# A second tile for the transposed probabilities, three copies with a second engine to run on, and a new order for the first 800 tasks

## The chip, the cores and the metric

The kernel runs on one core of a Trainium2 chip. The metric is the device time of that core in microseconds: 615.44 us, the median of three runs before the change (614.84 to 616.58).

## The reference, cut to what matters

Block attention with a local window and block summaries, followed by a two-layer feed-forward net with softplus. `q`, `k`, `v` are 4 x 8 x 768 x 64 in fp32.

```python
k_sum = k.reshape(B, H, nb, 32, D).max(axis=3)      # 24 block summaries of the keys
v_sum = v.reshape(B, H, nb, 32, D).mean(axis=3)
scores_l = where(|i - j| < 16, scale * q @ k.T, -1e9)
scores_s = scale * q @ k_sum.T + log(32)
a = softmax(concat[scores_l, scores_s])
x = (a @ concat[v, v_sum]).transpose(...).reshape(3072, 512)
h = x @ w_in                                        # 512 x 2048
out = softplus(h) @ w_out                           # 2048 x 512
```

## The kernel before, in words

The 3072 tokens are twelve chunks of 256, taken in six groups x of two chunks. All matrix products of the net run as three products of rounded fp32 halves (a high part and a low part of each operand), so every weight and every x is split once into "high" and "low". The 2048 hidden features f are 16 tiles of 128. The first pass takes tiles 0 to 7 for groups 0 to 4, the last group takes all 16, then tiles 8 to 15 follow for groups 4 to 0.

The kernel body does not run its work directly. It adds 2052 numbered tasks to a list; each task has an engine, a function that emits its instructions and the tiles that it reads and writes. `SEQUENCE` is a string written out by hand with all task numbers, and `Order.issue` emits the tasks in that order. Each engine then runs its own tasks in exactly this order, and waits where a tile is not ready or not yet free. A letter behind a number picks another way for the task: "a" is the first entry of its list `ways`, "b" the second. The SP queue issues all DMAs, also in this order.

An attention unit is two head pairs of one chunk. The first group has four, called U1 to U4 here in the order of their numbers: U1 is tasks 59 to 72, U2 73 to 86, U3 97 to 110, U4 111 to 124. Each runs these tasks, given with U1's numbers: scores (59, PE, line 650), mask with the row's maximum (60, DVE, L663), exp with the row's sum (61, ACT, L671), inverse of the sum (62, DVE, L678 and L679), normalise (63, on POOL or DVE at L684, or on ACT at L687), two transposes on PE (64 and 66, L704), two copies of the transposed probabilities into the tile `pT` (65 and 67, L708), values (68, PE, L749), and for each head pair the high part of x (69 and 71, L777) and its low part (70 and 72, L781). All units share one `pT`. The units of later groups (U5 is tasks 298 to 315, U6 323 to 340) go another way from the normalised probabilities to `pT`: a block transpose on DVE into the tile `tb` (303 in U5, L717), a DMA out to memory (304) and four DMAs back into `pT` (305 to 308).

Beside this the weights are prepared in place, tile by tile: load, magnitude (L951 on DVE, L954 on ACT), clamp, shift, sign (L958 to L966, DVE), tail (L972 on ACT, L975 on DVE), add_tail (L980, POOL), high (L984) and low (L991). Tasks 132 to 167 are the four 512-column pieces of weight pair 0 (w_in from 132 and 150, w_out from 141 and 159, nine tasks each); 168 to 186 are pair 1, 187 to 205 pair 2 and 206 to 224 pair 3, each a w_in and a w_out piece of 1024 columns. Task 50 is the mean of the values' blocks (L441).

The first products of the net are tasks 225 and 226 (the two halves of hidden tile f0, L1077), 234 and 235 (f1), 241, 242, 248 and 249 (f2 and f3); 227, 228 and 229 are the softplus of f0 (rounded, exact and the rest, L1227, L1231, L1235), and 230 to 233 its four projections into the output tiles (L1242). 27 tasks (3 to 29, `warm`, L1316) multiply the identity by itself, two matmul records each; nothing reads their result.

The lines that the change touches:

```python
pT = buffer([P, NG * NU * P], F32, "pT", bufs=1)
order.add(ACT, act(NU * P, True), transposed, [pt], [(pT, g)])
order.add(ACT, act(CH, True), high, [xo], [(*key, 0, i)])
order.add(ACT, act(DM, True), mean, [total], [kept])
```

Of the kernel before, what the change touches and what calls it, by code (L numbers as in the profile page):

```python
# [10 lines left out]
F32 = mybir.dt.float32  # L11
# [3 lines left out]
AF = mybir.ActivationFunctionType  # L15
# [135 lines left out]
94 316 100 189 25 148a 190 26 151a 152 27 114 90 101b 155 149 153 92 95 191 68 71 69 154 78 91 96 299 80 156 79 81 177  # L151
82 300 178 157a 72 323 127 358 129 158 70 115a 160 102 341 104 83 345 128 85 161 103 86 162 301 84 105 192 28 29 106
164 107 109 302a 163 116 118 225 117 165 119 108 183 303 304 324 120 193 166 234 343 123 121 325 206 349 122 347 124
110 226 235 167a 342 292 353 346 179 180 475 326 476a 365 227 228 181 236 229 327b 237 230 344a 231 182 351 241 242
194 297 293 296 305 238 184 350 211 248 328 243 249 348a 244 185 232 294 250 186 233 251 239 366 352 308 329 307 306
367 295 240 245 383 196 252 246 197 354 130 195 207a 247 368 309 330 317 208 369b 479a 209 390 210 331 333 332 255 256
370 310 474 314 355 212 391 198a 320 322 262 392 213a 199 253 318 321 319 202a 200 371 214 215 393 263 482 254 201 257
216 258 264 259 203 265 334 394b 501b 266 269 359 360 356a 372 375 373 270 335 502b 505 357 204a 276 395 205a 500 363
217a 277 483 361 374 362 364 260 218 396 219 221 271 220 261 272 278 273 508 279 222 280 376 526 484 267 384 223a 397
400 399 224 268 398 387 312a 274 389 385 337 527b 313a 528b 485 388 339 486a 377 379 275 284 282 281 386 381 340a 648  # L160
487 382a 338a 488 509 283 510 652 126 401 315 533 380 536 402a 404a 406a 288 407 554 405 408 489 491 492 490 477 478
480 409 555b 410 556 649 511 417 512a 561a 411 285 286a 656 412 418 481 513 413 419 514 537 420 403 650 660 424 421
538 414 415 425 426 564 493 665 666b 427 667 651 289a 539 540a 541 416 515 503 504 517 422 516 506 428 423 518 494a
429 507 565 566 542 87 654 125 653 672 567 568a 430 431 432 433 519 543 529 434 657 435 675 520 524a 569 436 693 544
676 677 678 438 439 437 530 525 661 655 534 531 570 546 545 440 532 535 441 694 662 700a 442 445 446 496a 658 522 523
695 497a 443 447 448 449 679a 547 557 571 562 558 559 560 680 703 722 548 721 574 550 551a 704 573 563 572 723 659
663a 452 705 706 453 444 450 88 681 451 454 726a 707 457 455 456 729 747 748 752a 749b 575 576 578 498a 499a 459 708
552 580 553a 581 460 682 336 378 685 579a 582 461 462 463 495 583 730 458 584 585 287 465 290 668 670 466 464 311 683
664 467 468a 591 592 471a 897 469 731 586 669 587 709 674 684 598 732 733 755 577 593 588 734 840b 589 901 599 594 595
605 756 846 839 671 606 841b 600 601 607 602 849 472a 608 673 868a 895 609 686 590 596 735 869 710 757 758 612 613 696  # L170
699 898a 698 614 597 615 687 689 712 603 521 701 697 713 604 616 691a 711 702 899 714 867 896 903 715 619 759 620 724
760 850 610 851 736 725 739 737 611 900 852 874a 626 853 621 470 622 719 627 738 623 628 904 617 629 727 761 728 740
741 877 905 907 762 688 902 618 630 765 633 764 912 745 750 624 625 634 913b 753 751 631 763 754 632 854 717 906 766
878 914a 919 879 855 922 880 842 690 635 743a 856 940 908 636 848 473 881b 843 637 746 718a 720a 767a 771a 692 744
941b 857 847 845 769a 638 942a 772 859 770a 844 773 782 642a 774 858 775 882 776 923 883 783 784 947a 777 639 785 640
950 860 884 641 924 886 1035 786 645a 789 549 861a 870 887 646a 1034 643 873 1036 909 778 885 790 925 926a 779 875 876
871 927 951 796 780 952 791 1039a 953 797 792 781 862 742 793 910 787 954 798 799 863 872 788 794 928 888 800 1366 915
911 955 956 1042 889a 1043 1044 1045 1046 929 918 803 804 647 1047 810 811 805 812 921 931 916 1059b 813 806 1063a 865
920 932 1060 807 930 1058 795 801 802 808 644 917 1066 866 814 768 1067 893a 1083 933 943 957 934a 960 949 809 815 816
936 938a 1084a 946 1089a 864a 939 935 817 818 1068 948 1082 891a 892 819 820 944 824 825 821 958 959 822 826 945 1048  # L180
1069 961 827 962 1500 716 1092 1070a 1037 937 823 964a 1367 894a 966 828 1049 963 1052 829 1038 1041 1051 1071 833 967
965a 831 1109 968 832 969 970 1108 977 1040 971 890 836a 1115a 837 978 979 830 1050 980 1072 1093 1110 972 981 1118
1053 1094 834a 1061 973 1054 974 1095 1056 1057 1064 1062 1368a 1096 1055 1073 975 1065 1076 984 985 986 987 991 992
988 993 1097 1119 994 1075 838 976 998 999 1000 1501a 995 1074 1001 1002 1098 982 1077 1372 835 1369 1120 1121 1078
1080 1506 983 1085 1081 1099 1091 989 990 1079 1005 1006 1502 1100 1012 1007 1102 1376 1008 1122b 996 1086 1088 1087
1090 1009 997 1123 1013 1101 1103 1014 1124 1015 1106 1003 1111 1004 1113 1016 1112 1019 1373 1104 1125 1020 1379 1010
1021 1117 1128 1022 1023 1127 1107 1116 1114 1503 1011 1126 1017 1510 1105 1507a 1018 1025 1026 1129 1024 1130 1132
1131 1028 1031 1133 1134 1135 1143 1136 1144 1027 1137 1145 1138 1192 1029 1139 1150 1151 1146 1193a 1147 1157 1210
1152 1032 1158 1211 1140 1212 1141 1194 1228 1195 1196 1213 1159 1153 1142 1160 1154 1161 1215a 1148 1214 1233 1201
1164 1149 1171 1172 1165 1229 1206a 1377a 1216 1197 1155 1033 1156 1217 1162 1219 1247 1030 1202a 1230 1231 1203 1232  # L190
1220a 1204 1205 1207 1198 1166 1234 1167 1173 1199 1163 1237 1218 1168 1174 1200a 1175 1178 1179 1248a 1249 1235 1185
1180 1181 1224a 1250 1169 1238 1170 1186 1251 1285 1236 1266 1182 1243 1252 1239a 1240 1221 1176 1241 1208 1242 1187
1253 1188 1177 1189 1302 1267a 1268 1183 1303 1222 1309 1244 1269 1290a 1310 1184 1256 1304 1305 1223 1306 1190 1311
1191 1257 1254 1271 1275 1225 1312 1313 1316 1226 1378a 1317 1323 1209 1270 1245 1255 1272 1227 1318 1319 1324 1307
1262 1325 1308 1273 1246 1314 1315 1276 1320 1286 1287a 1326 1277a 1258a 1327 1274 1330 1288 1259 1260 1281 1331 1261
1332 1333 1334 1337 1278 1263 1321 1338 1279 1344 1339 1380a 1345 1340 1322 1280 1341 1289 1351 1381 1352 1294a 1346
1374 1264 1375 1347 1265 1382 1328 1329 1370 1348 1371 1335 1336 1385 1282 1283 1383 1353 1354 1355 1386 1387a 1508a
1291 1384 1342 1388 1391 1389a 1392 1390 1394 1393 1395 1396 1399 1397 1284 1343 1398 1295 1292 1400 1403 1404 1401
# [33 lines left out]
def kernel(  # L232
# [111 lines left out]
    class Sums:  # L344
# [69 lines left out]
        def declare_first_values(self):  # L414
# [1003 lines left out]
```

## Time and profile before

| what | value |
|---|---|
| median of three runs | 615.44 us |
| span of the profiled execution, first to last instruction | 612.5 us |
| median less that span | 2.9 us |
| PE busy | 601.8 us (98%) |
| DVE, ACT, POOL busy | 383.8, 342.6, 179.3 us |
| granted TensorE clock, mean | 1.000 |

The span is that of one profiled execution; no time of its own beyond the span is given for it, and 2.9 us lie between the span and the median of the timed runs. PE counts as busy while a matmul waits in its pipeline, so 98% is not 98% of its rate: how much work a stretch holds is read from the number of matmuls in it.

### The profile page before, as it was taken

The numbers are of one execution on the slowest core, as the hardware profiler recorded it, in microseconds if no ns is written. First come the engines' busy times: TensorE is split into PE (matmuls) and PEld (weight loads), VectorE is DVE, ScalarE is ACT, GpSimd is POOL, SyncE is SP. The second block draws the span as 40 slices with busy tenths as digits, with TensorE's granted clock in tenths as the row PEclk, the third lists the DMA queues.
The fourth block names the chain that finished last, engine by engine and source line by source line (L and its number), as shares of the span: only waits on it lengthen the run. The fifth ranks groups of instructions, "written<-read, shape, count | busy, mean of one in ns | idle before, by whom it ended". The sixth has DMA issues, their size and how long they took to land.

```text
span 612.5 us, 12196 instructions
## 1 busy us (share of the span) xinstructions
PE 601.8 (98%) x4557; PEld 505.8 (83%) x4557; DVE 383.8 (63%) x990; ACT 342.6 (56%) x847; POOL 179.3 (29%) x179
## 2 busy tenths in 40 slices
PE   8899999999999999999999999999999999999997
PEld 7577878888788788888888888899898989899996
DVE  4999988765566665442235689854765665554543
ACT  4999998876778656576265986432213222133211
POOL 4324242244115132210003553572411236012000
PEclk9999999999999999999999999999999999999999
DMA  8989868988768476655428510041060043030121
GB/s 293 314 274 289 249 229 251 290 244 281 250 208 268 158 214 221 222 195 192 135 74 272 205 70 1 1 155 52 1 225 16 1 130 112 34 104 1 47 92 68
DMA packets 69130, 98.62 MB, mean 161 GB/s; under 512 B 6000, under 2 KB 47824, under 8 KB 68304
## 3 DMA queue, kind: packets, MB, share of 16 engines
q1 hardware_dynamic: 69072, 97.85, 49.9%
q8 instruction: 36, 0.59, 0.4%
q14 instruction: 22, 0.18, 0.1%
HBM read 67.11 MB, written 28.31 MB: 156 GB/s over the span
## 4 chain that ended last, share of the span: by engine, by line
PE 77%; ACT 10%; DVE 7%; DMA 2%; issue 2%; POOL 1%; SPq 0%; DVEq 0%; ACTq 0%; POOLq 0%
PE po L1242 36%; PE ph L1077 16%; PE hx L1117 10%; PE hy L1117 7%; PE xo L749 3%; PE sc L650 3%; PE warm L1316 2%; DMA raw<-w_out_dram 2%; ACT sp L671 1%; ACT raw L972 1%; ACT L1227 1%; ACT t L954 1%; DVE sp L663 1%; ACT L954 1%; ACT ph L1231 1%
## 5 line engine op out<-in xcount | busy, mean ns | idle before, releaser
L1242 PE MATMUL po<-w,gh 128*128 128x512 f32 x766 | 203.0, 392 | 0.7 <-DVE w L991 0.5
L1242 PEld LDWEIGHTS po<-w,gh 128*128 128x128 f32 x766 | 140.8, 188 | 30.3 <-DVE w L991 1.0
L1077 PE MATMUL ph<-xw,w 128*128 128x512 f32 x672 | 161.7, 391 | 0.0
L1077 PEld LDWEIGHTS ph<-xw,w 128*128 128x128 f32 x672 | 125.2, 188 | 27.2 <-issue 0.5
L1242 PE MATMUL po<-w,gl 128*128 128x512 f32 x383 | 114.5, 392 | 0.5 <-DVE gl L1235 0.5
L1242 PEld LDWEIGHTS po<-w,gl 128*128 128x128 f32 x383 | 70.7, 188 | 15.4 <-DVE gl L1235 0.9
L671 ACT ACTIVATE sp<-sp,nm 128x120 f32<-128x120 f32 x192 | 73.1, 386 | 4.2 <-DVE nm L663 4.0
L980 POOL TENSOR_TENSOR t<-t,raw 128x1024 int32<-128x1024 int32 (+1 forms) x20 | 40.7, 2042 | 111.1 <-DVE t L966 85.9
L1227 ACT ACTIVATE gh<-hx 128x512 fp32r<-128x512 f32 x20 | 12.0, 600 | 107.6 <-DVE hx L1127 107.6
L1235 DVE TENSOR_TENSOR gl<-ph,gh 128x512 fp32r<-128x512 f32 x56 | 38.4, 689 | 50.4 <-ACT ph L1231 50.1
L1227 ACT ACTIVATE gh<-ph 128x512 fp32r<-128x512 f32 x56 | 33.4, 598 | 38.3 <-PE ph L1077 38.1
L821 POOL TENSOR_TENSOR x<-r,x 128x512 fp32r<-128x512 f32 x23 | 30.5, 1338 | 53.2 <-DVE x L814 43.5
L663 DVE CUSTOM_DVE_ANT_0 sp<-sc,added 128x120 f32<-128x120 f32 x192 | 40.8, 277 | 4.1 <-PE sc L650 3.1
L671 ACT ACTIVATION_READ_ACCUMULATOR sp<-sp,nm 128x1 f32 x192 | 36.7, 191 | 0.0
L1117 PE MATMUL hx<-x,w 128*128 128x256 f32 x240 | 35.7, 285 | 0.0
L1117 PE MATMUL hx<-x,sw 128*128 128x256 f32 x240 | 35.5, 284 | 0.0
L1117 PEld LDWEIGHTS hx<-x,w 128*128 128x128 f32 x240 | 32.9, 190 | 2.1
L1117 PE MATMUL hy<-x,sw 128*128 128x256 f32 x240 | 34.4, 284 | 0.0
L1227 ACT ACT_TABLE_LOAD x23 | 29.5, 1283 | 6.2 <-PE ph L1077 5.8
L1231 ACT ACTIVATE ph<-ph 128x512 f32<-128x512 f32 x56 | 33.0, 591 | 0.0
L1117 PEld LDWEIGHTS hx<-x,sw 128*128 128x128 f32 x240 | 32.0, 190 | 0.8
L1117 PEld LDWEIGHTS hy<-x,sw 128*128 128x128 f32 x240 | 31.2, 191 | 0.2
(120 smaller groups left out, 831.7 us busy)
## 6 DMA issues: line engine op xcount, KB each, us to landing
squares<-tb SPq DMA_DIRECT2D x20, 512.0 KB
pT<-squares SPq DMA_DIRECT2D x80, 128.0 KB
raw<-w_out_dram SPq DMA_DIRECT2D x16, 512.0 KB
kf<-kT_dram SPq DMA_DIRECT2D x16, 384.0 KB
raw<-w_in_dram SPq DMA_DIRECT2D x6, 1024.0 KB
q<-qT_dram SPq DMA_DIRECT2D x20, 256.0 KB
part<-ob SPq DMA_DIRECT2D x10, 512.0 KB
out_dram<-ob SPq DMA_DIRECT2D x10, 512.0 KB
```

What stands on the lines that cost most here:

```text
L650: nc.tensor.matmul(unit(g * NU + h * NPAIR + i)[r * QW:(r + 1) * QW, k0:k1], lhsT=q[rows, w * QW:(w + 1) * QW], rhs=k[rows], start=True, s ...
L663: nc.vector.tensor_tensor_reduce(out=sp()[:, n], in0=unit(n), in1=added()[:, kinds.index((lows[w], lows[w + 1]))], scale=-SCALE, scalar=FL ...
L671: nc.scalar.activation(sp()[:, n], sp()[:, n], AF.Exp, bias=nm()[:, n:n + 1], scale=-1.0, accum_out=ss()[:, n:n + 1],)
L749: nc.tensor.matmul(xo()[h * D:(h + 1) * D, g * CH + w * QW:g * CH + (w + 1) * QW], lhsT=v[:, h * D:(h + 1) * D], rhs=queries(g, w, h), sta ...
L821: engine.tensor_tensor(to(1), a(), to(0).bitcast(F32), op=ALU.subtract)
L980: nc.gpsimd.tensor_tensor(a, a, word(0, I32), op=ALU.add)
L1077: nc.tensor.matmul(ph(), lhsT=lhs(part, cc), rhs=xw[cc][0]()[:, xw[cc][1], a], start=cc == 0 and n == 0, stop=cc == NCC - 1 and n == 2,)
L1117: nc.tensor.matmul(to()[:, half], lhsT=lhs(wa, cc), rhs=of_x(xa)[:, cc * CH:(cc + 1) * CH], start=cc == 0 and m == 0, stop=cc == NG - 1 an ...
L1227: nc.scalar.activation(gh(), all_of(), AF.Softplus)
L1231: nc.scalar.activation(all_of(), all_of(), AF.Softplus)
L1235: nc.vector.tensor_sub(out=gl(), in0=all_of(), in1=gh().bitcast(F32))
L1242: nc.tensor.matmul((to or po[t])()[:, c0:c1], lhsT=a()[:, t * P:(t + 1) * P], rhs=w2()[:, part, i2 * DM + c0:i2 * DM + c1], start=(f == f0 ...
```

## The change

Four edits. The tile of the transposed probabilities takes the ring of `tb` for the second chunk of the first group (U2 and U4), and stays in the ring of `pT` for U1 and U3. The copies out of the transposes, the high part of x in the first group (and in the last, which runs through the same code) and the mean of the values may also run on DVE. The first 800 places of `SEQUENCE` hold the same 800 tasks in another order and partly with other letters; the 1252 places behind them are the same.

```diff
-        pT = buffer([P, NG * NU * P], F32, "pT", bufs=1)
+        pT = buffer([P, NG * NU * P], F32, "pT", "tb" if by_pe and i else "pT", 1)
...
-                def transposed(g=g, pt=pt):
-                    nc.scalar.copy(out=pT()[:KS, g * NU * P:(g + 1) * NU * P], in_=pt()[:KS])
-                order.add(ACT, act(NU * P, True), transposed, [pt], [(pT, g)])
+                def transposed(copy, g=g, pt=pt):
+                    copy(out=pT()[:KS, g * NU * P:(g + 1) * NU * P], in_=pt()[:KS])
+                order.add(ACT, act(NU * P, True), lambda f=transposed: f(nc.scalar.copy), [pt], [(pT, g)], ways=[Way(DVE, dve(NU * P), lambda f=transposed: f(nc.vector.tensor_copy))])
...
-            order.add(ACT, act(CH, True), high, [xo], [(*key, 0, i)])
+            order.add(ACT, act(CH, True), lambda f=high: f(nc.scalar.copy), [xo], [(*key, 0, i)], ways=[Way(DVE, dve(CH), lambda f=high: f(nc.vector.tensor_copy))])
...
-            order.add(ACT, act(DM, True), mean, [total], [kept])
+            def mean_by_vector(): nc.vector.tensor_scalar_mul(kept()[KW:KS], total()[KW:KS], 1.0 / BLOCK)
+            order.add(ACT, act(DM, True), mean, [total], [kept], ways=[Way(DVE, dve(DM), mean_by_vector)])
```

The beginning of the order, old and new (places 0 to about 110 of the old and 0 to 240 of the new; the rest up to place 800 is changed in the same way):

```diff
-131 0 132 51 2 3 30 32 4 55 5 168 6 7 38 93 40 8 9 133a 34 10 137 134 11 135 12 13 14 31 15 16 136 42 44 33 138 59 1
-139 17 60 140 18 61 19 89 169 73 36 170 141 171 173 46 291 52 62 172 63b 74 39 41 48 174 43 45 187 75 35 150 64 37 66
-175a 97 65 67 176 53 76 98 77 47 99 56 57 49 142 143 111 144 50 145 146 112 54 147 113 58 188 159 20 21 22 23 24 298
...
+0 3 132 137 1 4 5 6 7 8 9 131 2 30 31 32 10 11 12 13 14 15 133a 134 135 136 138 139 140a 55 51 33 59 60 61 141 142 143
+144 146a 145 147 16 17 18 19 20 73 74 168 169a 170 171 172 173 174 75 62 63b 175 176a 38 40 21 39 41 34 35 42 44 46 36
+48 43 45 47 49 50 76 37 77a 64 65a 93 89 97 98 150 151a 155a 152 153 148a 149a 154 156 22 23 66 111 112 24 25 99 100
+101 67 113 52 90 57 53 56 291 54 58 68 71a 72 78 79a 159 164a 160a 69 80 81 298 26 114 115 299 300 82 85 83 70 102 27
+28 104 29 103 105 161 187 157 192 162 188 163 189 84 301 86 190 302a 191 158 91 94 127 95 130 96 92 106 116 118 117
+119 120 303 165 166 167a 107 193 109 121 110 177 128 178 183 316 323 324 206 123 122 108 124 179 343 344 341 342 345
+475 346 325 326 225 234 226 227 228 229 207 235 236 237 238 208 180 209 181 182 184 358 292 293 304 297 129 194 211
...
```

Of the first 800 tasks 72 change their engine. Up to task 226 these are: from ACT to DVE 65, 71, 79 (copies) and 146, 155, 164 (tails); from ACT to POOL 101 (U3's normalise); from DVE to POOL 115 (U4's normalise), 140, 149, 176 (lows); from POOL to DVE 77 (U2's normalise); from DVE to ACT 157, 160, 169, 175. The mean (50) stays on ACT. All 27 `warm` tasks stay in the first 800.

## Rows read from the trace of the kernel before

**Rows 1.** The page: span and busy time by engine.
```profile
span 612.5 us, 12196 instructions
...
PE 601.8 (98%) x4557; PEld 505.8 (83%) x4557; DVE 383.8 (63%) x990; ACT 342.6 (56%) x847; POOL 179.3 (29%) x179
```
**Rows 2.** Windows: stretch, length, busy us (instructions) per engine, clock, DMA share, GB/s.
```profile
30.00:40.00 10.00, 8.63 (x179) 7.31 (x173) 9.93 (x35) 9.97 (x38) 1.29 (x1) 1.00 0.95 280
...
150.00:160.00 10.00, 10.00 (x45) 8.07 (x43) 4.71 (x23) 7.81 (x23) 0.96 (x1) 1.00 0.99 335
```
**Rows 3.** Waits of PE from 40 to 260 us: total, times, longest.
```profile
PE xo L749 <- DVE ob L1283: 0.5, 1, 0.5
```
**Rows 4.** Timeline of PE: start, us, instruction, count [idle before, releaser].
```profile
25.93 2.43 PE L1316 MATMUL warm<-ident 128*128 128x256 f32 x10
...
35.33 1.18 PE L749 MATMUL xo<-pT,first 120*64 120x64 f32 x32 [1.22 <-ACT pT L708]
...
50.53 0.73 PE L1242 MATMUL po<-w,gh 128*128 128x512 f32 x2 [0.15 <-ACT gh L1227]
...
51.75 0.50 PE L1242 MATMUL po<-w,gl 128*128 128x512 f32 x1 [0.49 <-DVE gl L1235]
...
59.56 1.98 PE L1242 MATMUL po<-w,gh 128*128 128x512 f32 x8
```
**Rows 5.** Chain of waits, 0 to 60 us: start, us, what.
```profile
12.09 0.20 DVE sp L663
...
24.63 1.37 PE sc L650 x38
```
**Rows 6.** ACT by line and shape, 0 to 110 us: busy, mean ns, idle before.
```profile
L687 ACT ACTIVATE sp<-sp,ss 128x120 f32<-128x120 f32 x40 | 12.0, 387 | 0.6 <-ACT t L954 0.3 <-DVE ss L679 0.3
...
L708 ACT COPY pT<-pt 120x512 f32<-120x512 f32 x8 | 4.4, 609 | 0.0
...
L972 ACT ACTIVATE raw<-raw 128x512 int32<-128x512 uint32 x4 | 2.8, 688 | 0.0
...
L954 ACT ACTIVATE t<-raw 128x1024 f32<-128x1024 f32 x3 | 3.4, 1143 | 0.0
...
L984 ACT CAST w<-t 128x1024 fp32r<-128x1024 f32 x2 | 2.1, 1042 | 0.0
```
**Rows 7.** DVE by line and shape, 0 to 110 us.
```profile
L684 DVE TENSOR_TENSOR sp<-sp,ss 128x960 f32<-128x960 f32 x4 | 4.6, 1154 | 0.1
...
L991 DVE TENSOR_TENSOR w<-t,w 128x1024 fp32r<-128x1024 f32 x5 | 6.1, 1219 | 0.1
...
L1283 DVE COPY ob<-po 128x512 f32<-128x512 f32 x2 | 1.4, 682 | 0.0
...
L975 DVE TENSOR_SCALAR raw<-raw 128x1024 int32<-128x1024 uint32 x1 | 0.7, 689 | 0.0
```
**Rows 8.** POOL by line and shape, 0 to 110 us.
```profile
L684 POOL TENSOR_TENSOR sp<-sp,ss 128x960 f32<-128x960 f32 x1 | 1.8, 1790 | 3.0 <-DVE ss L679 3.0
...
L991 POOL TENSOR_TENSOR w<-t,w 128x512 fp32r<-128x512 f32 x1 | 1.3, 1307 | 0.0
```
**Rows 9.** Timeline of DVE: the first maximum and U1's first mask.
```profile
8.16 0.95 DVE L352 TENSOR_REDUCE ks<-kf 128x24 f32<-128x768 f32 x1 [2.03 <-DMA kf<-kT_dram]
...
11.60 0.28 DVE L663 CUSTOM_DVE_ANT_0 sp<-sc,added 128x120 f32<-128x120 f32 x1 [1.02 <-PE sc L650]
```
**Rows 10.** Timeline of ACT: the first exp of U3 and of U5.
```profile
23.16 0.39 ACT L671 ACTIVATE sp<-sp,nm 128x120 f32<-128x120 f32 x1 [0.39 <-DVE nm L663]
...
35.63 0.43 ACT L671 ACTIVATE sp<-sp,nm 128x120 f32<-128x120 f32 x1
```
**Rows 11.** Timeline of DVE and POOL: one operation beside POOL and without it.
```profile
13.83 0.69 DVE L951 TENSOR_SCALAR t<-raw 128x1024 uint32<-128x1024 uint32 x1
...
27.69 1.29 POOL L980 TENSOR_TENSOR t<-t,raw 128x512 int32<-128x512 int32 x1 [2.85 <-ACT raw L972]
...
28.30 1.23 DVE L951 TENSOR_SCALAR t<-raw 128x1024 uint32<-128x1024 uint32 x1
```

More of the change, by code (lines that the diff above doesn't have):

```diff
@@ new lines @@
+269 276 270 271 272 273 260 482 500 501 88 277 261 395 396 483 376 384 387 388 389 385 221 222 223a 224 397 398 399
+400 386 267 268 312a 313a 337a 278 279 502b 280 505a 508 484 315 377 527b 528b 381 379 380a 648 382a 485 486a 487 509
+488 526 274 275 283 288 281 282 339 338a 401 402a 404a 477 480 478 406a 407 405 340a 408 417 409 510 533a 285 536 555
+418 284 511 512a 513 410 411 286a 412 413 489 492 491 490 481 493 419 561a 420 652 421 650 514 651 503 506 494 498a
+537 289a 538 539 540 541 414 424 431 425 415 416 426 432 433 427 422 554 556 564 87 125 504 515 434 428 435 565 566
@@ new lines @@
+1190 1311 1191 1257 1254 1271 1275 1225 1312 1313 1316 1226 1378a 1317 1323 1209 1270 1245 1255 1272 1227 1318 1319
+1324 1307 1262 1325 1308 1273 1246 1314 1315 1276 1320 1286 1287a 1326 1277a 1258a 1327 1274 1330 1288 1259 1260 1281
+1331 1261 1332 1333 1334 1337 1278 1263 1321 1338 1279 1344 1339 1380a 1345 1340 1322 1280 1341 1289 1351 1381 1352
+1294a 1346 1374 1264 1375 1347 1265 1382 1328 1329 1370 1348 1371 1335 1336 1385 1282 1283 1383 1353 1354 1355 1386
+1387a 1508a 1291 1384 1342 1388 1391 1389a 1392 1390 1394 1393 1395 1396 1399 1397 1284 1343 1398 1295 1292 1400 1403
@@ new lines @@
+1517a 1482 1487 1519 1520a 1644 1518a 1521a 1522 1524 1523 1525 1528 1526 1527 1531 1532 1535 1529 1530 1533 1635
+1636a 1483 1484 1534 1638a 1491 1537 1490 1488 1536 1544 1545 1538 1539 1546 1549 1552 1641 1493 1497 1555 1550a 1553
+1498 1551 1558 1489 1554 1642a 1556 1540 1494 1560 1643 1559 1561 1541 1562 1563 1564 1557 1565 1569 1570 1566 1542
+1543 1571 1547 1548 1574 1575a 1580 1577 1578 1576 1581 1579 1582 1585 1583 1587 1584 1586 1567 1588 1589 1650a 1590
+1591 1647 1568 1594 1595 1596 1572 1599 1605 1600 1602 1608 1601 1573 1603 1609 1610 1604 1651 1652 1606 1612 1613
@@ new lines @@
+1607 1592 1611 1593 1614 1648a 1619 1645a 1639a 1499 1615 1646a 1620 1597 1653a 1778 1616 1621 1649 1654 1655a 1656
+1657 1658 1659 1660 1662 1665 1661 1768 1663 1667 1771 1598 1666 1668 1669 1664 1671 1672 1673 1670 1678 1679 1617
+1680 1626 1769a 1495 1770 1774 1772a 1618 1630 1775 1622 1683 1776a 1684 1685 1627 1623 1686 1687 1689 1692 1777a 1688
+1690 1628 1694 1696 1624 1693 1695 1784a 1773a 1902 1903 1698 1904 1912 1913 1914 1625 1699 1674 1697 1691 1703 1700
+1631 1704 1675 1676 1705 1708 1711 1632 1709a 1677 1712 1714 1781a 1715 1719 1710 1720 1717 1713 1718 1721 1723 1681
@@ L228 @@
+1809 1810 1839 1811 1815 1842 1848 1843a 1845 1844 1846 1847 1849 1851 1853 1850 1852 1854 1857 1816 1917 1855 1856
+1835 1858 1859 1862 1836 1863 1864 1867 1870 1911a 1873 1869 1926 1868a 1871 1874 1878 1872 1876 1879 1877 1767 1924a
+1927 1929a 1928a 1882 1883 1880 1921 1875 1840 1881 1925a 1884 1841 1930 1860 1887 1931a 1922a 1888 1889 1932 1935
+1933a 1934 1938 1936 1943 1941 1937 1894 1898 1945 1861 1865 1939 1946 1940 1944 1942 1947 1954 1866 1948 1955 1885
[5 rows of a table added]
 """
@@ L774, in of_bank, with high @@
                 return xo()[:, g * CH:(g + 1) * CH]
-            def high(of_x=of_x, of_bank=of_bank):
-                nc.scalar.copy(out=of_x(0), in_=of_bank())
-            order.add(ACT, act(CH, True), high, [xo], [(*key, 0, i)])
+            def high(copy, of_x=of_x, of_bank=of_bank):
+                copy(out=of_x(0), in_=of_bank())
+            order.add(ACT, act(CH, True), lambda f=high: f(nc.scalar.copy), [xo], [(*key, 0, i)], ways=[Way(DVE, dve(CH), lambda f=high: f(nc.vector.tensor_copy))])
             def low(of_x=of_x, of_bank=of_bank):
```

118 lines of the change are left out of this document (45 added, 73 removed), and 11 rows, old and new, of the table SEQUENCE.

## The prediction

> **What bounds the kernel now.** I read the page first, then the busy time by stretch, then the timelines of PE, ACT and DVE up to 60 us. PE is busy for 98% of the span [rows 1], and from about 60 us on that is real work: 45 matmuls of 512 columns in 10 us, one per 0.222 us [rows 2], and from 40 to 260 us no single wait of PE is longer than 0.5 us [rows 3]. The front is different: from 30 to 40 us PE shows 8.6 us busy, but DVE and ACT are at 9.93 and 9.97 of 10 us [rows 2]. Attention of the first group and the weights' preparation stand there in two full queues, and PE waits (1.22 us at 35.33 for a copy on ACT) or multiplies the identity by itself, as the ten records at 25.93 show [rows 4]. All 27 such tasks stay in the new order, and all 800 tasks do the same work. So the change can only alter the time that PE loses before it is saturated, and every microsecond won there should reach the end, since what follows place 800 is the same and is paced by PE. I take as the goal post the moment at which PE has done all of f0 and f1's hidden halves, U6's scores, the next scores (365), the hidden halves of f2 and f3 and f0's four projections. In the kernel before that is 59.56 [rows 4].
>
> **The change part by part: sums.** Up to task 226 ACT gives up two copies (0.609 each), a cast of half that width (0.4, an estimate between a copy of 512 columns and nothing, nearer the copy for its fixed part), three tails (0.688 each) and U3's normalise (8 of 0.30 = 2.4, from 12.0 us for 40), together 6.1 us. It takes on a magnitude and a high of 1024 columns (1.143, 1.042) and one of each of 512 (taken as 0.6 each), 3.4 us [rows 6]. Net 2.7 us less; starts overlap by about 0.1, so 2.4. DVE takes on U2's normalise (1.154), two copies from PSUM (the nearest is the 128x512 copy, 0.682), a cast (0.4) and three tails (0.689 for 1024 columns, so 0.4 each), 4.1 us. It gives up a low of 1024 (1.219) and two of 512 (0.65 each, half and a bit), U4's normalise (1.154) and four cheap weight steps (0.69 twice and 0.42 twice), 5.9 us [rows 7]. Net 1.8 less. POOL takes two normalises for one (1.79 more) and three lows (1.307 twice and, by its width, 2.4), 6.8 us more [rows 8]; in the stretch from 30 to 40 it was busy for 1.29 us only [rows 2]. So by sums the front could be 1.8 to 2.4 us shorter. Whether it is depends on the order.
>
> **The walk through the new order.** *Start.* Before, DVE had clamp and shift of the first weight behind it when it waited 2.03 us for the first key tile (8.16), and U1's mask began at 11.60 [rows 9]. Now the keys are issued ahead of one q tile, but DVE's first task is the maximum of those keys, and clamp and shift come after. The two effects nearly cancel: I take U1's mask at 11.75 (11.2 if the keys land over 1 us earlier, 12.2 if no earlier). *U1 to U3.* A row of eight masks takes 1.6 us (0.20 each) [rows 5], eight exps 3.1 (0.39 each) [rows 10]. ACT: U1's exps 12.05 to 15.15, magnitude and tail of pair 1 (1.1 each, less overlap) to 17.25, U2's exps to 20.35, U1's normalise 2.4 to 22.7. On PE the scores of U3 now stand behind U1's first transpose, so behind that normalise: transpose to 23.1, scores (1.37 [rows 5]) to 24.5, U3's first exp at 24.85. Before it was 23.16 [rows 10]: 1.7 us later. *U4 and U5.* U4's scores need the tile free, so follow U3's masks (26.1) and end at 27.5; five weight steps on DVE (2.2) put U4's mask at 28.3, its exps at 28.65 to 31.75. Here the sums pay: U3's normalise is on POOL, so ACT has only 1.5 us of small work before U5's exps, 33.2 against 35.63 [rows 10]. *To the products.* U5's exps to 36.3, four casts and copies 1.75, two weight steps 1.65, U4's copies 1.05: 40.7. U4's values end at 41.8 (1.1, from the 1.18 of such a group [rows 4]), U6's scores at 43.2. DVE reaches U5's block transpose at about 42; it writes `tb`, which U4's probabilities now hold until 41.8, so this new wait costs 0 to 0.4; behind it stand U6's mask and the lows that f0's second half reads, done at 46.4. PE: first halves of f0 and f1 (6 x 0.222 each) to 45.9, a wait to 46.5, second halves to 49.2, scores 365 to 50.5, f2 and f3 5.3 to 55.9, four projections 2.7 to 58.5. Spread of the 0.222 (some groups run at 0.227) adds 0.3: 58.6. Against 59.56 that is 0.9 to 1.0 us won. Nearly all of it is one place: before, PE came to f0's projections at 50.53 after a wait of 0.15, did two matmuls (0.44 us of work) and stood until 51.75 for DVE's rest, about 0.9 lost [rows 4]; now the 5.3 us of f2 and f3 lie between the softplus and its projections and cover it. If that cover were gone, the gain is nil.
>
> **A rule against it.** DVE's magnitude of 1024 columns took 0.69 us alone and 1.23 beside a POOL operation that had begun 0.6 us before it, 0.54 more [rows 11]. The walk meets three DVE operations of this kind beside POOL's new ones, so 0 to 1.6 us on DVE's side. Half of that is hidden in the wait for `tb`; I put 0.1 into the sum and the rest into the range. The Trainium skill (SBUF — State Buffer, Who interferes with whom) says that the two engines share a pair of ports under an exclusive lock, and that whoever comes second is blocked for the whole instruction. The trace agrees for this operation; if every operation of POOL met DVE so, the 6.8 us more on POOL would undo the whole gain of the sums.
>
> **After the goal post.** Tasks change their engines there too, but ACT and DVE have slack there (4.71 and 7.81 of 10 us at 150 [rows 2]) and PE's remaining visible waits are small, such as 0.5 for one output copy [rows 3]. I take 0.4 us gained of that 0.5 (0 to 0.5; a loss is rival 2), since the weights' loads come earlier in SP's queue. SP is moved past a new stall: load 343 must wait for U4's values (41.8) and holds the next keys behind it; they are needed by DVE at 47, about 4 us after their issue (the first key tile came at 8.16 with the whole start's loads beside it [rows 9]). I count nothing for it; if they land 1 us late, 365 and all behind it are 1 us late.
>
> The sum is made on the profiled execution: 612.5 - 0.9 (59.56 to 58.6, the 0.1 put in) - 0.4 = 611.2. The median of the runs lies 2.9 us above that span, so 614.1.
>
> **Rivals.** (1) *The engine sums come through in full.* For it: ACT and DVE are full queues, so work taken off them should shorten them, 2.4 us, and the 0.9 at 51 goes as well: 3.3 less, 612.1. Against it: U3's exps, 1.7 late by the walk. It decides by U3's first exp lying at or before 23.2. (2) *PE gives the gain back*: what is won before 59.56 is lost in new waits of the later units, since 1 us is less than one row of exps: 615.4. For it: every unit from U5 on is laid out anew. Against it: PE has whole hidden tiles in hand there. (3) *Slower: U3's late start is not caught up.* Its 1.7 us run on in full, because U3's and U4's normalises now both pass through POOL, behind the new low of pair 1 (2.4), and U4's waits for U3's, 1.79 more. f0's second half then starts 3.5 later than the 46.5 of the walk, at 50.0, the goal post is at 62.1, 2.5 behind the 59.56, and the time is 617.9. From 47.5 on that start is a loss, from 49.3 one that can be measured. Against it: POOL was idle most of the time, so three new operations should find room.
>
> **How the numbers follow.** A measurement of this kernel can tell about 0.3% (1.85 us) from no change: below 613.6 is faster, above 617.3 slower. The cases overlap with these bounds as follows. Forecast 614.1, chance 0.44, own range 612.9 to 615.3; the start (0.4 each way) and POOL's ports make it: 0.14 of it below 613.6. Rival 1, 0.26, all faster. Rival 2, 0.12, 0.02 of it slower. Rival 3, 0.18, 0.16 of it slower. Faster 0.40, same 0.42, slower 0.18. The range for 8 in 10 leaves out the best part of rival 1 and the worst of rival 3: 611.4 to 617.4.
>
> **What would show it.** In the profile after: U1's mask near 11.75; U3's first exp near 24.8 and U5's near 33.2; f0's second half at 46.5, with a wait of PE before it; no wait of PE between 50 and 56; the projections of f0 done near 58.6; the clock still 1.00, as before [rows 2]. I am wrong if PE's matmuls per stretch between 60 and 230 us fall (new waits), if U3's exp is not late, or if the tail of the program differs by other than a shift.

## The result: 620.2 us against 616.0, slower

The kernel after took 620.23 us (median of four runs, 619.2 to 623.0), the kernel before 616.01 beside it (four runs, 614.8 to 617.5). The ratio is 1.0079, 95% interval 1.0050 to 1.0107. (Ratios here compare fast runs with fast runs and need not be the quotient of the two medians.) The forecast was 614.1, in a range up to 617.4: sign and size were wrong. In this document "the kernel after" is the changed kernel, "the kernel before" the unchanged one.

In the page of the profile after, the span is 4.9 us longer than in [rows 1] (by the trace; the rounded spans differ by 5.0), and the clock's line (tenths of full speed in 40 slices) has an 8 where that of the kernel before has nines only:

```profile
span 617.5 us, 12175 instructions
PE 605.2 (98%) x4557; PEld 506.2 (82%) x4557; DVE 384.2 (62%) x997; ACT 338.7 (55%) x828; POOL 190.9 (31%) x184
PEclk9989999999999999999999999999999999999999
```

Over the whole span ACT was busy 3.9 us less and POOL 11.6 more, the way that was counted up to task 226; DVE, counted 1.8 less, was busy 0.4 more. The stretches that answer to [rows 2] show where PE stood (columns as there):

```profile
35.00:40.00 5.00, 2.95 (x45) 2.38 (x44) 4.93 (x15) 5.00 (x18) 2.33 (x2) 0.99 0.88 254
40.00:45.00 5.00, 4.58 (x92) 4.01 (x90) 5.00 (x5) 4.09 (x9) 2.37 (x2) 0.67 0.92 296
45.00:50.00 5.00, 4.32 (x28) 3.62 (x29) 4.72 (x22) 3.51 (x18) 3.41 (x3) 1.00 1.03 314
```

From 35 to 40 us PE was busy for 2.95 of 5 us, and in the next 5 us the granted clock was 0.67. PE's timeline there, beside [rows 4]:

```profile
35.93 0.60 PE L1316 MATMUL warm<-ident 128*128 128x256 f32 x2
38.58 1.15 PE L749 MATMUL xo<-pT,first 120*64 120x64 f32 x32 [2.05 <-DMA first<-v]
39.66 1.76 PE L704 MATMUL pt<-ident,sp 128*120 128x128 f32 x8
41.35 1.98 PE L749 MATMUL xo<-pT,first 120*64 120x64 f32 x32
45.68 0.32 PE L650 MATMUL sc<-kf,q 64*64 64x96 f32 x3 [1.10 <-issue]
46.09 5.75 PE L1077 MATMUL ph<-xw,w 128*128 128x512 f32 x24
53.08 5.74 PE L1077 MATMUL ph<-xw,w 128*128 128x512 f32 x24
61.47 1.15 PE L749 MATMUL xo<-pT,v 120*64 120x64 f32 x32
```

Three things are to be seen. U3's values waited 2.05 us for the loads of the mean's rows (`load_sums`, tasks 92 and 96). Behind that wait, at the lower clock, eight transposes took 1.76 us (1.09 at full clock) and U4's values 1.98 (U3's took 1.15). And within U6's scores PE stood 1.10 us more, waiting for no engine and no tile that the profile names ("issue"). The goal post, the end of f0's four projections, is where PE's next work begins: U5's values at 61.47, instead of 59.56, where the kernel before begins a projection.

To follow the loss further I use one measure for all kernels: the start of a values group, less the work of all PE tasks issued ahead of it, each kind of task at one price. Against the kernel before, the kernel after is 1.8 us ahead at U2's values, 0.1 behind at U3's, 1.8 behind at U5's (309) and U6's (334), 4.6 behind at values 860 (about 216 us), and stays there to within 0.02 up to the last values. The remaining 0.3 of the 4.9 lies behind those. So there are two losses: 1.8 us in the front, and 2.8 between 60 and 216 us. The front's is a loss of 3.6 between U2's values and U5's: the wait of 2.05, 1.5 at the lower clock and the stall of 1.10 make 4.65, less 1.0 that the kernel before loses there itself (0.15 and 0.49 of it in [rows 4]).

### The profile page after: what moved, and what is told of

Same layout as the page of the kernel before. It is cut to its first block, busy times and chain, and to the rows that moved or that the text cites. A ratio compares the mean times of both kernels' runs of the same rounds, so it can differ in the third digit from the quotient of the medians.

```text
span 617.5 us, 12175 instructions
## 1 busy us (share of the span) xinstructions
PE 605.2 (98%) x4557; PEld 506.2 (82%) x4557; DVE 384.2 (62%) x997; ACT 338.7 (55%) x828; POOL 190.9 (31%) x184
## 4 chain that ended last, share of the span: by engine, by line
PE 79%; ACT 7%; DMA 6%; SPq 3%; DVE 3%; issue 1%; POOL 1%; DVEq 0%; ACTq 0%
PE po L1242 38%; PE ph L1077 18%; PE hx L1117 9%; PE hy L1117 7%; PE xo L749 4%; PE sc L650 3%; DMA raw<-w_out_dram 2%; DMA squares<-tb 1%; ACT t L954 1%; DMA first<-qT_dram 1%; DMA first<-v 1%; ACT sp L671 1%; DMA st<-v_hp_dram 1%; ACT raw L972 1%; ACT L954 1%
## 5 line engine op out<-in xcount | busy, mean ns | idle before, releaser
L980 POOL TENSOR_TENSOR t<-t,raw 128x1024 int32<-128x1024 int32 (+1 forms) x20 | 42.3, 2121 | 92.9 <-DVE t L966 62.7
```

Of the source, the lines that this page charges most:

```text
L980: nc.gpsimd.tensor_tensor(a, a, word(0, I32), op=ALU.add)
```

## The experiments

All times are medians; "front" is the lag behind the kernel before at values 309 and "later" what comes on top from values 334 to 860, both by that measure, from one profiled execution of each. (f1 and h3 lose another 1.2 and 2.7 us from values 309 to 334, which neither column holds.) "Excursions" are the times PE goes from wide matmuls (512 columns) to the narrow ones of attention and back between 334 and 860.

| kernel | us (before beside it) | ratio, 95% interval | front | later | excursions |
|---|---|---|---|---|---|
| after | 620.23 (616.01) | 1.0079 (1.0050 to 1.0107) | 1.8 | 2.8 | 22 |
| a2, after again | 621.00 (615.09) | 1.0073 (1.0046 to 1.0100) | 7.0 | 2.3 | 22 |
| e1, sums first | 619.78 (616.02) | 1.0056 (1.0035 to 1.0078) | 2.4 | 3.2 | 22 |
| e2, fill the wait | 621.02 (616.02) | 1.0078 (1.0049 to 1.0108) | 1.9 | 4.1 | 22 |
| n1, fill more | 621.14 (614.53) | 1.0098 (1.0063 to 1.0133) | 3.8 | 3.3 | 22 |
| f1, DVE first | 623.16 (614.98) | 1.0140 (1.0117 to 1.0163) | 6.0 | 4.5 | 22 |
| g1, short adds | 619.62 (615.09) | 1.0068 (1.0048 to 1.0087) | 2.4 | 3.4 | 22 |
| g0, short adds, before | 614.88 (615.09) | 0.9992 (0.9974 to 1.0009) | 0.3 | -0.4 | 12 |
| c1, code only | 617.14 (614.98) | 1.0036 (1.0021 to 1.0051) | 2.0 | 0.6 | 12 |
| v1, f2 and f3 first | 616.59 (615.09) | 1.0006 (0.9988 to 1.0025) | 1.2 | 0.2 | 12 |
| h1, front new | 622.41 (616.02) | 1.0101 (1.0071 to 1.0131) | 8.5 | 1.0 | 12 |
| h3, front old | 625.48 (616.02) | 1.0146 (1.0117 to 1.0175) | 7.5 | 2.4 | 22 |
| s1, split | 618.92 (614.98) | 1.0067 (1.0050 to 1.0085) | 0.7 | 4.2 | 22 |
| j1, joined | 625.70 (614.98) | 1.0175 (1.0156 to 1.0195) | 3.1 | 6.6 | 15 |

### The load that U3's values waited for (e1)

```diff
 SP's queue
-54 58 159 187 91 94 127 95 130 96 92 177
+54 58 96 92 159 187 91 94 127 95 130 177
```

> The kernel after, with U3's two loads of the mean's rows (tasks 92 and 96) issued right behind those of U1 and U2 (58), ahead of two weight loads and U3's values' own loads. Theory A (a wait for these loads, and the clock's fall behind it, is the first half of the loss): PE's wait of 2.05 us ahead of U3's values is under 0.5, the granted clock stays at 1.00 from 39 to 44 us, the goal post is at about 58.6 to 59.5 instead of 61.47, and the time is 2 to 3 us below that of the kernel after, 617 to 618. Rival B (the front's loss is taken up by slack later): the wait goes, but the time stays within 1 us of the kernel after, 619.5 to 621. Rival C (the loads moved back are late in their turn): a new wait of PE, DVE or ACT for a weight, and no gain.

PE's timeline of e1:

```profile
37.93 1.17 PE L749 MATMUL xo<-pT,first 120*64 120x64 f32 x32 [0.65 <-ACT pT L708]
40.45 1.17 PE L749 MATMUL xo<-pT,first 120*64 120x64 f32 x32 [0.34 <-ACT pT L708]
42.95 3.24 PE L1077 MATMUL ph<-xw,w 128*128 128x512 f32 x13
48.02 3.82 PE L1077 MATMUL ph<-xw,w 128*128 128x512 f32 x11 [1.84 <-DVE xw L781]
```

The wait for the load is gone, and U3's values start 0.65 us earlier, not 2.05: PE now waits for ACT's copy of the probabilities, which is done 0.65 before the load was. The products start at 42.95, 3.1 us earlier than in the kernel after, and then wait 1.84 for DVE's lows of the first group. Behind that wait the clock is at 0.71 from 50 to 55 us (11 products in 3.82 us, 2.5 at full clock), and the 24 products end at 51.8 in both kernels. Theory A got the wait right and its price wrong, and the time is Rival B's; the second limit, DVE, is what Theory A left out.

### DVE beside POOL (f1, g1, g0)

In the kernel after, these DVE operations began beside one of POOL's (first DVE, then POOL):

```profile
20.67 1.50 DVE L678 TENSOR_SCALAR ss<-ss 128x8 f32<-128x8 f32 x1
30.12 0.88 DVE L678 TENSOR_SCALAR ss<-ss 128x8 f32<-128x8 f32 x1
32.49 0.96 DVE L975 TENSOR_SCALAR raw<-raw 128x512 int32<-128x512 uint32 x1
38.53 0.94 DVE L678 TENSOR_SCALAR ss<-ss 128x8 f32<-128x8 f32 x1
42.71 1.76 DVE L991 TENSOR_TENSOR w<-t,w 128x512 fp32r<-128x512 f32 x1
44.40 1.23 DVE L717 STREAM_TRANSPOSE tb<-sp 128x1024 f32<-128x1024 f32 x1
47.84 1.08 DVE L781 TENSOR_TENSOR xw<-xo,xw 128x256 fp32r<-128x256 f32 x3
```

```profile
29.67 1.29 POOL L980 TENSOR_TENSOR t<-t,raw 128x512 int32<-128x512 int32 x1
37.81 1.63 POOL L980 TENSOR_TENSOR t<-t,raw 128x512 int32<-128x512 int32 x1 [2.11 <-issue]
42.63 1.29 POOL L991 TENSOR_TENSOR w<-t,w 128x512 fp32r<-128x512 f32 x1 [3.20 <-ACT w L984]
43.89 2.84 POOL L980 TENSOR_TENSOR t<-t,raw 128x1024 int32<-128x1024 int32 x1
```

The operation on eight columns takes 0.15 us alone. At 38.53 it took 0.94 and ended at 39.47; POOL's add had ended at 39.44. Over the five operations up to 47 us the extra is 1.35, 0.73, 0.54, 0.79 and 1.08, together 4.5 us; in the kernel before it is 0.30 and 0.54, of which [rows 11] shows the second. So DVE lost 3.65 us more to POOL, against the 1.8 us of work that the prediction freed it from: 1.85 late by these two. Its last lows of the first group (47.84) indeed come 2.0 us later than in the kernel before, 0.28 of it in a wait for U6's scores:

```profile
45.82 1.08 DVE L781 TENSOR_TENSOR xw<-xo,xw 128x256 fp32r<-128x256 f32 x3
```

The block transpose at 44.40 ran beside POOL's add at its usual length. The Trainium skill (SBUF — State Buffer, Who interferes with whom) says that DVE's two-port modes and its operations with two inputs in SBUF contend with GpSimd for a whole instruction, and others do not; the rows agree with it, down to the lows of L781, whose one input lies in PSUM and which kept 0.42 us beside POOL.

The first attempt to free DVE moved work in the queues:

```diff
 on top of e1; DVE's queue
-... 302a 191 158 303 110 324 122 108 124
+... 302a 158 191 303 110 122 108 124 324
 POOL's queue
-165 167a 193
+165 193 167a
 PE's queue
-365 241 248 242 249
+241 248 242 249 365
```

> The kernel after with U3's load_sums early as in e1_sums_first, and DVE's queue relieved: the low of the weight part 158 ahead of 191, POOL's low 167 behind its 193 (so that no POOL operation runs when DVE comes to 158), the lows 122, 108 and 124 of the first group ahead of U6's mask, and on PE the scores 365 behind the first halves of f2 and f3. Theory A (DVE's queue, which POOL's operations hold up, sets the start of f0's second half; the load of U3's rows only hid that): DVE's 158 takes 0.7 us instead of 1.76, PE's wait of 1.84 ahead of f0's second half is under 0.5, the clock stays at 1.00, the goal post lies at 58.5 to 59.5 instead of 61.5, the time 617.5 to 618.5. Rival B (another queue stands right behind: U6's mask, the next keys' maxima or the copies on ACT): a new wait of PE of 1 us or more between 46 and 60 us, goal post over 60.5, 619.5 to 620.5.

It was a miss: 623.2. The lows came at 46.50 instead of 47.22 in e1, U6's mask behind them at 47.51 instead of 45.60, and PE waited 2.58 us for DVE's rest of a softplus ahead of f2's and f3's halves. Rival B, at another place of DVE's own queue, and slower than its 619.5 to 620.5. Next I left POOL's work out instead of moving DVE's:

```diff
 on top of e1; POOL's queue: 165 193 167a
-                nc.gpsimd.tensor_tensor(a, a, word(0, I32), op=ALU.add)
+                k = 64 if pair < 3 else n
+                nc.gpsimd.tensor_tensor(a[:, :k], a[:, :k], word(0, I32)[:, :k], op=ALU.add)
```

> As e1_sums_first (U3's load_sums early), and POOL's add of the low words (the operation named add_tail) works on 64 of its columns for the first three pairs of weights, so most of that addition is left out; POOL's low 167 goes behind its 193. DVE's own work is the same. Theory A (DVE waits for POOL: in the kernel after operations of DVE that began beside one of POOL's were longer by 1.35, 0.73, 0.55, 0.79 and 1.08 us up to 47 us, 4.5 together, against 0.85 in the kernel before, and that made f0's second half late): the first, second, fourth and fifth of these go, 3.95 us; PE's wait of 1.84 ahead of f0's second half is under 0.5, the clock stays at 1.00 there, the goal post lies near 59 instead of 62.0 in e1_sums_first, the time is 616.7 to 617.5. Rival B (DVE is not what bounds the front): DVE is shorter, the goal post stays above 61, 619 to 620.

> The kernel before with the same adds of POOL cut to 64 columns (most of that addition left out), as the control for g1_short_adds. Theory A: only 0.85 us of DVE's time in the front hangs on POOL here, so the goal post moves from 59.56 by 0 to 0.9 and the time is 615 to 616. Rival (POOL's adds are on the path by themselves, whatever DVE does): over 1.5 us less.

DVE's rows in g1, then PE's and the stretch from 30 us:

```profile
40.73 0.16 DVE L678 TENSOR_SCALAR ss<-ss 128x8 f32<-128x8 f32 x1
44.14 0.68 DVE L992 TENSOR_TENSOR w<-t,w 128x512 fp32r<-128x512 f32 x1
```

```profile
30.24 0.69 PE L749 MATMUL xo<-pT,first 120*64 120x64 f32 x16 [2.18 <-DMA first<-v]
45.37 6.07 PE L1078 MATMUL ph<-xw,w 128*128 128x512 f32 x24
```

```profile
30.00:35.00 5.00, 4.52 (x84) 4.01 (x88) 2.22 (x6) 3.11 (x13) 2.21 (x2) 0.70 1.03 307
```

The mechanism holds: with POOL's adds short, DVE's operations are back at 0.16 and 0.68, and the 24 products run with 0.3 us lost instead of 1.84. The time does not follow: 619.6, as e1 and as Rival B has it. U1's values, for which PE was ready at 28.06, now waited 2.18 us for their own load_sums, and the clock fell behind them. In the kernel before the same cut changes nothing (0.9992, interval 0.9974 to 1.0009), as theory A says: little of DVE hangs on POOL there, and the adds alone are not on the path.

### The clock behind a wait (e2, n1, a2)

e2 put three of the identity's multiplications (27 to 29) just ahead of U3's values.

> The kernel after, with three of the tasks that multiply the identity by itself (27 to 29, 0.47 us of PE each) moved to just ahead of U3's values, into the wait of 2.05 us; no load is moved. If the clock's fall comes from PE standing still: the wait shrinks to about 0.6, the load still lands at 38.5, but the granted clock stays at 1.00 behind it, and 1.0 to 1.7 us of the loss go: 618.5 to 619.2. If the clock's fall has another cause: 0.50 from 40 to 43 us as in the kernel after, and 620.2.

This told nothing. The three ran as soon as PE reached them, the values came at 39.64 instead of 38.58, the wait was 2.16 us, and the clock was 0.50 from 41 to 44 us. n1 therefore adds work:

```diff
+            if task.index == 106:
+                for _ in range(4):
+                    self.tasks[29].ways[0].run()
```

> The kernel after with eight more multiplications of the identity by itself (four times the work of task 29, 0.47 us each, 1.9 us together) on PE right ahead of U3's values, in the wait for their load. If PE's standing still brings the clock down and the clock carries most of the front's loss: the wait of 2.05 us becomes under 0.6, the clock stays at 1.00 from 38 to 45 us, eight transposes of U3's neighbour take 1.1 instead of 1.76 and U4's values 1.15 instead of 1.98, and U4's values are issued 0.7 us earlier; the goal post comes 1 to 1.7 us earlier, 618.5 to 619.2. If the loss is the waits of other engines (DVE's lows at 48 us): the clock stays up as well, but PE waits 1 to 2 us ahead of f0's second half, and the goal post and the time stay within 0.7 us of the kernel after, 619.8 to 620.9.

PE in n1, and the stretch in which the clock fell:

```profile
37.37 2.32 PE L1319 MATMUL warm<-ident 128*128 128x256 f32 x10
39.70 1.15 PE L752 MATMUL xo<-pT,first 120*64 120x64 f32 x32
40.78 1.09 PE L707 MATMUL pt<-ident,sp 128*120 128x128 f32 x8
42.16 1.18 PE L752 MATMUL xo<-pT,first 120*64 120x64 f32 x32 [0.29 <-ACT pT L711]
45.90 0.33 PE L653 MATMUL sc<-kf,q 64*64 64x96 f32 x4 [1.56 <-issue]
```

```profile
45.00:50.00 5.00, 4.10 (x29) 3.40 (x30) 4.89 (x23) 3.32 (x17) 4.65 (x4) 0.75 0.88 283
```

With PE multiplying through the wait, the clock stayed at 1.00 up to 45 us and transposes and U4's values took 1.09 and 1.18 instead of 1.76 and 1.98. So in this pair of executions the clock's fall followed from PE's standing still. But then U6's scores stood 1.56 us on "issue", the clock fell behind that, and the 24 products took 7.36 us instead of 5.75. The front did not gain: neither of the two outcomes that I had written down. (Its 3.8 in the table counts the added multiplications as loss, 1.9 us; without them it is 1.9, as in the kernel after.)

> The kernel after once more, unchanged, to see how much of its front repeats. If the wait of 2.05 us for U3's load_sums, the clock's fall behind it and the 1.10 us of issue within U6's scores belong to the kernel, all three come again to 0.5 us and the goal post is at 61 to 62; if they are of one execution, the goal post differs by over 1 us. The time: 619 to 621 either way, and the same 22 excursions of PE from wide to narrow matmuls between the values 334 and 860.

The kernel after, run and profiled again: its front lost 7.0 us in this execution instead of 1.8. U3's values came at 41.15, the "issue" stall came at the same scores, and the clock fell twice, at 41 to 44 and at 51 to 54 us. So wait, stall and fall belong to the kernel, and their sizes to the execution:

```profile
41.15 1.98 PE L749 MATMUL xo<-pT,first 120*64 120x64 f32 x32 [2.31 <-ACT raw L972]
49.23 0.32 PE L650 MATMUL sc<-kf,q 64*64 64x96 f32 x3 [1.93 <-issue]
```

ACT's operation named there was long done, so another, most likely the load, was the last to come. Of the eight timed runs of a2, the four with a mean clock of 0.999 or 1.000 took 618.7 to 621.0 us, the four with 0.993 to 0.997 took 621.0 to 624.1. The clock is thus part of the loss and of its spread, and a loss of 3.6 us and more remains without it.

What PE waited for on "issue" the timelines do not name, but the page has a queue of its own for loads of instructions, the same line in both kernels:

```profile
q8 instruction: 36, 0.59, 0.4%
```

These are 36 loads of 16 KB. Counted in PE's matmuls, every stall of 0.25 us or more on "issue" in the fifteen profiles lies right ahead of the 347th, the 473rd or the 599th, 126 apart, whatever task that is: the 599th in after (1.10), a2 (1.93), n1 (1.56) and h1 (0.87), the 473rd in a2 (0.79), e2 (0.68) and h1 (0.49), the 347th in h3 (2.21) and in the kernel before (0.25). In n1 eight more multiplications moved the stall eight matmuls forward within U6's scores. Each stall ends 1.2 to 1.7 us after one of these loads has landed (44.18, then 45.68 in the kernel after), and in no profile does one of the three matmuls start sooner than 1.1 us behind its load. So PE most likely stood for its own next instructions. No run moved such a load, so this is read from the traces and not tested, and why the load came late is not shown.

### The new tile and the order of f2 and f3, each alone (c1, v1)

c1 has the code of the kernel after with the order and the letters of before.

```diff
-303 304 324 120
+120 303 304 324
```

> The code of the kernel after with the order and the letters of the kernel before; only U4's values (120) stand two places earlier in the global order, ahead of U5's block transposes (303, 304) and U6's mask (324), as the shared tile demands. Theory A (the whole loss is in the order, none in the second tile of transposed probabilities): 616.0, U2's copies a little earlier or the same, first 60 us as in the kernel before to 0.3 us. Rival B (the block transpose now waits for U4's values): goal post up to 1 us late, 617.

```profile
44.85 1.25 DVE L717 STREAM_TRANSPOSE tb<-sp 128x1024 f32<-128x1024 f32 x1 [1.59 <-ACT raw L972]
```

```profile
48.23 2.80 PE L1077 MATMUL ph<-xw,w 128*128 128x512 f32 x11 [1.68 <-DVE xw L781]
```

U4's values ended at 44.74 in c1, and the block transpose started at 44.85, after 1.59 us of waiting; in the kernel before it ran at 42.92. The lows behind it are late by as much, and PE waits 1.68 for them. The new tile by itself costs about 2 us in the old order (ratio 1.0036, 1.0021 to 1.0051). In the kernel after, U4's values end at 43.33 and DVE comes to the transpose at 44.40: there the wait is nothing.

```diff
 the kernel before, PE's queue
-230 231 241 242 248 249 232 233
+241 242 248 249 230 231 232 233
```

> The kernel before with one part of the change alone: on PE f0's projections 230 and 231 go behind the first halves of f2 and f3 (241, 242, 248, 249). By the prediction's step for that place (two waits of 0.15 and 0.49 at 50 to 52 us are covered by 5.3 us of products): both waits go, the goal post lies 0.5 to 0.9 earlier, about 58.9, the time 615 to 615.5. Rival (another wait stands behind, for the exps of f2 or for U5's values): goal post at 59.5, 616.

```profile
51.90 3.02 PE L1077 MATMUL ph<-xw,w 128*128 128x512 f32 x12 [1.34 <-DVE gl L1235]
55.14 3.06 PE L1077 MATMUL ph<-xw,w 128*128 128x512 f32 x12 [0.23 <-DVE gl L1235]
```

The rival: the two waits ahead of the projections (0.15 and 0.49, [rows 4]) went, and the halves of f2 and f3 now wait 1.57 us for DVE's rests of f0 and f1. The front is 1.2 later. By the ratio the time cannot be told from that of the kernel before, though the medians lie 1.5 us apart, the way the front does.

### The loss between 60 and 216 us (h1, h3, s1, j1)

One excursion in the kernel before and two in the kernel after, in PE's timelines (first before, then after):

```profile
118.61 2.43 PE L1077 MATMUL ph<-xw,w 128*128 128x512 f32 x10
120.97 1.15 PE L749 MATMUL xo<-pT,v 120*64 120x64 f32 x32
122.05 1.05 PE L650 MATMUL sc<-k,q 64*64 64x120 f32 x32
123.03 2.12 PE L1242 MATMUL po<-w,gh 128*128 128x512 f32 x8
```

```profile
119.05 1.05 PE L650 MATMUL sc<-k,q 64*64 64x120 f32 x32
120.03 1.21 PE L1242 MATMUL po<-w,gl 128*128 128x512 f32 x4
121.25 1.15 PE L749 MATMUL xo<-pT,v 120*64 120x64 f32 x32
122.33 1.88 PE L1242 MATMUL po<-w,gh 128*128 128x512 f32 x7
```

Before, values and scores stand together. After, a projection of four matmuls lies between: from 120.03 to 121.25 is 1.22 us for four that take 0.91 in a run (0.227 each). From start to start, the last wide matmul ahead of a narrow one takes 0.318 and the first wide one behind takes 0.336 to 0.341: 0.09 and 0.11 more, 0.205 an excursion. Between values 334 and 860 the kernel before has 12 excursions (2.44 us so lost) and the kernel after 22 (4.52). That is 2.1 of the 2.8 us. The second to seventh wide matmuls behind a return are a little slow too: together 0.25 us in the kernel before and 0.60 in the kernel after, another 0.35.

h1 and h3 cross the orders: h1 has the new front (254 places) and the old rest, h3 the old front and the new rest, both cut behind f0's projections (233).

> The kernel after up to the goal post (its first 254 places, through f0's projections), then the remaining tasks in the order and on the engines of the kernel before. Theory A (half of the loss, about 2.7 us, comes from the later part of the new order, between 60 and 200 us): goal post still near 61.5, then no further drift, 617.9. Rival B (the later drift follows from how the front ends: late engines, loads behind each other): 620.2 as the kernel after. Rival C: the seam itself costs, over 621.

> The kernel before up to task 233 in its order, then the remaining tasks in the order and on the engines of the kernel after. Theory A (the later part of the new order costs about 2.7 us by itself): goal post at 59.6, 618.7. Rival B (the later part is as good, the whole loss comes from the front): 616.0.

As times both are spoiled by the seam: PE waited 2.9 us for a weight in h1 and 4.8 us ahead of U5's values in h3, so the seam costs, as Rival C of h1 has it. Behind it they say what was asked: 12 excursions and 1.0 us more with the old rest, 22 and 2.4 with the new.

s1 is the kernel before with 11 such pairs split:

```diff
 the kernel before, PE's queue, three of the 11
-309 390 255          -508 376 267          -564 493 416
+309 255 390          +508 267 376          +564 416 493
```

> The kernel before with 11 neighbouring pairs of scores and values on PE between 60 and 230 us taken apart: the second of each pair goes behind the next task of PE's queue. All else is as before. Theory A (0.2 us per change between narrow and wide matmuls): 2.2 us more lost by the values 860, 618.2. Rival B (such changes are free, the drift comes from the moved engines): 616.0.

It became slower, by 0.67% (0.50 to 0.85), which is 4.1 us: 22 excursions instead of 12 give 2.07 of that, and the list of PE's waits shows four that the shifts made, 1.3 together. Without any change in the engines' work, the splits' own switches cost what theory A said, and the shifts cost more on top.

j1 is the kernel after with pairs joined:

```diff
 the kernel after, PE's queue, three of the 7
-564 423 519          -675 437 547          -575 457 729
+423 564 519          +437 675 547          +457 575 729
```

> The kernel after with seven places of PE's queue changed between 60 and 215 us, so that scores and values of neighbouring units stand next to each other instead of with one projection between them (six scores go behind that projection, projection 457 goes ahead of values 575). Theory A (each change between the narrow matmuls of attention and the wide ones costs about 0.2 us, 0.09 going out and 0.11 coming back): 7 x 0.2 = 1.4 us less lost between the values 334 and 766, the front unchanged, 618.8. Rival B (the loss is in waits for late engines, which scores issued later make worse): no gain or a loss, 620 to 621.

15 excursions instead of 22 gave back 1.5 us by start-to-start times, as counted, and cost more in waits:

```profile
PE xo L749 <- DVE gl L1235: 3.5, 2, 1.7
PE xo L749 <- DMA pT<-squares: 1.4, 1, 1.4
```

Scores that come a projection later put exps, transposes and values of their unit behind too, which by these waits the new order cannot absorb. Rival B, at 625.7 even beyond its bound.

## Why the prediction was wrong, step by step

Two steps of the sum failed: the walk to the goal post, forecast at 58.6 and measured at 61.47, and "after the goal post", forecast at 0.4 gained and measured at 2.8 lost. For the second the main cause, ten more excursions, is measured, and s1 repeats it; for the first the parts are measured, but no run shows that one of them carries it.

*The start was right enough.* U1's mask began at 11.49 (forecast 11.75), U3's first exp at 25.18 (24.85), U5's at 34.02 (33.2; before 35.63 [rows 10]):

```profile
25.18 0.40 ACT L671 ACTIVATE sp<-sp,nm 128x120 f32<-128x120 f32 x1 [0.50 <-DVE nm L663]
34.02 0.40 ACT L671 ACTIVATE sp<-sp,nm 128x120 f32<-128x120 f32 x1 [0.76 <-DVE nm L663]
```

U3's normalise did leave ACT, and U2's values came 1.8 us ahead.

*"I put 0.1 into the sum" was the first mis-sized term.* DVE's hold-ups beside POOL, bounded by 0 to 1.6, measured 3.65 more than before. They ate the 1.8 us that DVE was freed from, and DVE was 2.0 late at the lows that f0's second half reads. In the kernel after PE was as late itself and did not wait for them (48.92, and f0's second half at 48.96); in e1, where PE was early, it waited 1.84. I had counted only three wide operations as exposed; three of the five held up work on eight columns, which cost 0.15 alone and waited for POOL's whole add. g1 and g0 show the mechanism. The list of moved tasks ahead of the prediction also leaves one out: 344, a sum of the next values, went from DVE to POOL and now stands ahead of 226. POOL ran it from 48.23, and a magnitude on DVE at 48.84 took 1.24 instead of 0.69.

*The walk left out the load that U3's values need.* It went from copies to values. PE got there 3.3 us earlier than before (36.5 against 39.84), the load was issued at the same time, 31.14 against 31.41, behind another megabyte of weights. Its own price was 0.65 us (e1); the clock's fall behind it took another 1.5 from transposes and U4's values. Yet with either taken away (e1, n1) the front did not come out earlier.

*"The clock still 1.00" was an assumption.* I priced no fall. All nine profiles with the new front show the clock at 0.50 somewhere between 32 and 55 us, behind waits of PE; of the six with the old front, four show none up to the program's end.

*A stall that I had no term for:* 1.10, 1.93 and 1.56 us of "issue" within U6's scores in after, a2 and n1, most likely for PE's own instructions. The kernel before has one of 0.25 us.

*The cover by f2 and f3* held in the kernel after, where PE waited for nothing between 50 and 56 us, as forecast. But its working (two waits of 0.64 simply covered) fails alone: v1 pays 1.57.

*The tile's wait*, put at 0 to 0.4, was 0 in the new order and 1.59 in the old (c1).

*"After the goal post", -0.4, failed by sign:* +2.8 between values 334 and 860. The wait of 0.5 did go (the lag falls by 0.6 at values 860), yet ten more excursions cost 2.1, the wide matmuls behind them 0.35, and all waits together some 0.3 more than before. I had read PE's order there as free because each task's work is the same, and PE's visible waits as the only loss: the 0.2 us of an excursion is no wait in the profile, and I had not looked at start-to-start times. That nothing changes behind place 800 was right.

Of the rivals, the third had the sign, with a mechanism that did not occur: POOL's normalises waited 0.41 and 0.74 us, and U3's late exp was caught up. That the front's loss has no single cause is the likeliest reading: load, DVE's lows, "issue" and the clock each stand within 1 or 2 us of the next, and taking one away (e1, g1, n1) moved the end by less than the runs can tell, while the same kernel's front varied by 5 us between two executions. Open are why PE's instructions came late, and what the front would take with all four gone; neither was tried. No version was faster than the kernel before.

## What to carry to other kernels

Before an order is changed on a busy engine, count how often its queue goes from one shape of work to another, by start-to-start times: a cost that no wait shows (0.2 us here), times ten, was nearly half of this change's loss. Where a front has several full queues, give a removed wait only the distance to the next one (0.65 of 2.05 us), and walk the DMAs with the engines. Moving work to POOL is priced by what DVE does meanwhile, smallest operations included.

## What the runs showed of the hardware

The granted clock went to 0.50, the 1.2 GHz level, for some 3 us (6.8 in h3) behind single waits of PE of 1.56 to 4.8 us, and in f1 and c1 behind three each of 0.2 to 0.8; it stayed at 1.00 up to 45 us when the wait was filled with multiplications (n1). It does not always fall: waits of 1.68 us in c1 and of 1.8 in s1 and g0 left it at 1.00. A DVE operation on eight columns was held up for 1.35 us by POOL. A switch of TensorE from 512-column to narrow fp32 matmuls and back cost 0.205 us at its two ends, in 12, 15 and 22 switches alike, and 0.02 to 0.03 more in the matmuls behind it. PE's stalls on "issue" lay at three fixed places of its program, each ending 1.2 to 1.7 us after a 16 KB load of instructions. And the same program lost 1.8 or 7.0 us up to U5's values in two profiled executions.
